# More unread matmuls in TensorE's gaps between the first tile's attention output and the first expert matmul

## The chip, the cores and the metric

One core of one Trainium2 chip. The metric is device time in microseconds (us). A "run" below is one execution of a kernel; each carries its time, its span from the first to the last instruction, and the mean granted clock of TensorE over that span (1.000 is full).

## The reference

Inputs are q, k, v of shape (8 batches, 8 heads, 576 tokens, 64), two norm weights, and two expert matrices of 512 x 2048 and 2048 x 512. In short:

```python
kv  = einsum('bhsd,bhse->bhde', k, v)            # no softmax
out = einsum('bhsd,bhde->bhse', q, kv)
x   = out / sqrt(mean(out**2, -1) + 1e-6) * g_norm      # per head, then heads side by side: 512 wide
xn  = (x - mean(x)) / sqrt(var(x) + 1e-6) * g_ln
y   = x + relu(xn @ w_ch1) @ w_ch2
```

The kernel works on 36 tiles of 128 tokens. A tile goes through: attention output (TensorE), squares and their sums, normalisation and centring (ScalarE, VectorE), a transpose to xT (TensorE), then the two expert products (TensorE).

## The kernel before: the parts that matter

The kernel first makes a plan: every piece of work is a step with an engine, an estimated length and its dependencies, and a small simulation in Python orders the steps. The instructions are then written in that order, with data dependencies guarded by semaphores. After the plan is made, the gaps of TensorE before the first expert matmul are filled with matmuls of a zeroed tile, whose result nobody reads:

```python
def idle_mm(count):
    if "idle" not in blk[0]:
        blk[0]["idle"] = psum.tile([128, 512], f32, tag="mm", name="idle_ps", bufs=BANKS["mm"])
    for _ in range(count):
        nc.tensor.matmul(blk[0]["idle"][:, 0:128], lhsT=blank, rhs=blank, start=True, stop=True)

order = run_plan()
first_mm = min(s.start for s in order if s.main)      # "main": the expert matmuls
pe_end, idle = WARM_FROM, {}
for s in order:
    if s.eng != "PE":
        continue
    if s.start <= first_mm:
        gap = s.start - pe_end                        # as planned, not as measured
        if s.start <= kv_first.start:
            idle[id(s)] = int(gap / 0.107 + 0.5)
        elif gap > 0.3 and not s.main and (s not in urgent or gap > 0.45):
            idle[id(s)] = int((0.6 if s not in urgent or gap > 1.2 else 0.45) * gap / 0.056)
    pe_end = s.start + s.occ
for s in order:
    if id(s) in idle:
        idle_mm(idle[id(s)])                          # unread matmuls just ahead of the step
    s.fn()
```

The first tile of q comes in slots. GpSimd issues their loads between those of the expert weights; the third slot is turned on TensorE (L427) between the two halves of the first tile's own transpose (L586):

```python
pool_load(("q", 0, 1), load_slot(qp[0], q, 0, 1), rate1)
load_w(0, 1)
pool_load(("q", 0, 2), load_slot(qp[0], q, 0, 2), rate1)      # the third slot
load_w(1, 1)
load_w(2, 1)
# ... cut ...
```

## Time and profile before

| | before |
|---|---|
| median of the first 3 runs | 293.42 us (292.99 to 294.43) |
| profiled span | 291.3 us |
| TensorE busy | 283.6 us, 97% |
| first expert matmul | 17.21 us |
| first long run of expert matmuls (64) | 18.95 us |
| unread matmuls | 90, of them 34 after 12 us |

A busy TensorE includes the unread matmuls and the drain of each burst, so its share says nothing about useful work in the first 17 us. The start times of the real matmuls, and the time in brackets before them, do.

### The profile page before, as it was taken

To read this page: it belongs to the slowest core of one execution; us is meant where nothing else is said; L and a number is where in the kernel's file an instruction comes from. 1 tells how busy PE (TensorE), PEld (TensorE's weight loads), DVE (VectorE), ACT (ScalarE), POOL (GpSimd) and SP (SyncE) were. 2 spreads that over 40 slices of the span, in tenths; PEclk is the share of its full clock that TensorE was granted. 3 is DMA by queue.
4 is the path that set the end of the run, shared out by engine and by line. 5 is a ranking of instruction groups with operands and counts; after the bars stand their busy time and mean duration, and the time that the engine had idled before them with its cause. 6 is when DMAs were issued, how large, how long until landed. Compare 5 with 4: busy or idle time off the path is not lost.

```text
span 291.3 us, 5178 instructions
## 1 busy us (share of the span) xinstructions
PE 283.6 (97%) x2046; PEld 162.1 (56%) x2074; DVE 165.0 (57%) x362; ACT 142.6 (49%) x288; POOL 66.7 (23%) x93
## 2 busy tenths in 40 slices
PE   8899999999999999999999999999999999999995
PEld 6779845977645445444544445444544444444444
DVE  2696039487973997557755775477557755320022
ACT  2379954788756512761276126612761177017400
POOL 8974231007309006304060406000000000000000
PEclk9999999999999999999999999999999999999999
DMA  6999999948999998996999399922101210120012
GB/s 95 184 198 205 204 199 179 244 83 96 182 222 94 170 138 141 169 181 140 160 96 188 76 201 96 180 73 92 54 18 56 90 54 18 56 88 20 2 72 73
DMA packets 108332, 35.60 MB, mean 122 GB/s; under 512 B 87059, under 2 KB 103827, under 8 KB 108308
## 3 DMA queue, kind: packets, MB, share of 16 engines
q0 software_dynamic: 72624, 18.35, 66.0%
q1 hardware_dynamic: 35540, 16.85, 25.9%
q8 instruction: 16, 0.26, 0.4%
q14 instruction: 8, 0.07, 0.1%
q10 hardware_dynamic: 144, 0.07, 0.1%
HBM read 36.70 MB, written 9.44 MB: 158 GB/s over the span
## 4 chain that ended last, share of the span: by engine, by line
PE 85%; DMA 7%; POOL 6%; issue 1%; ACT 0%; DVE 0%; POOLq 0%
PE mm_ps L670 41%; PE mm_ps L651 33%; DMA qb<-in_q_dram 7%; PE mm_ps L636 5%; PE out_ps L491 3%; PE kv_ps L468 2%; POOL qp L277 1%; POOL w L361 1%; POOL vb L256 1%; POOL kb L256 1%; PE xT_ps L586 1%; POOL w L363 1%; PE qT_ps L427 0%; ACT qp L407 0%; POOL identity masks.py:197 0%
## 5 line engine op out<-in xcount | busy, mean ns | idle before, releaser
L670 PE MATMUL mm_ps<-w,m 128*128 128x512 bf16 (+2 forms) x592 | 128.1, 367 | 0.7
L651 PE MATMUL mm_ps<-xT,w 128*128 128x512 bf16 x436 | 100.0, 379 | 0.6
L658 ACT ACTIVATE m<-mm_ps 128x512 bf16<-128x512 f32 x112 | 66.8, 597 | 50.8 <-PE mm_ps L651 48.5
L670 PEld LDWEIGHTS <-m 128*128 128x128 bf16 x608 | 57.2, 98 | 60.6
L651 PEld LDWEIGHTS <-w 128*128 128x128 bf16 x448 | 43.1, 98 | 48.8
L526 DVE TENSOR_REDUCE ss<-sq 128x8 f32<-128x512 f32 (+1 forms) x37 | 24.8, 669 | 48.2 <-ACT sq L517 48.1
L677 DVE SCALAR_TENSOR_TENSOR x<-mm_ps,rstd,x 128x512 f32<-128x512 f32 (+2 forms) x38 | 27.3, 720 | 40.6 <-PE mm_ps L670 40.5
L517 ACT ACTIVATE sq<-out_ps 128x512 f32<-128x512 f32 (+1 forms) x37 | 21.6, 584 | 45.4 <-PE out_ps L491 45.4
L636 PE MATMUL mm_ps<-xT,w 128*128 128x128 bf16 x512 | 30.6, 219 | 0.0
L636 PEld LDWEIGHTS <-w 128*128 128x128 bf16 x512 | 29.2, 98 | 0.9 <-DMA w<-in_moe_w_ch_dram 0.2
L579 DVE SCALAR_TENSOR_TENSOR xc<-x,mv,gl 128x512 bf16<-128x512 f32 (+1 forms) x38 | 27.3, 723 | 1.2
L521 DVE TENSOR_TENSOR xg<-out_ps,gn 128x512 f32<-128x512 f32 x34 | 23.2, 683 | 0.2
L757 POOL COPY mark<-xT 128x1 bf16<-128x1 bf16 x15 | 7.5, 497 | 58.1 <-DMA xT<-xc 52.6
L643 ACT ACTIVATE m<-mm_ps 128x512 bf16<-128x512 f32 x32 | 18.4, 596 | 3.1 <-PE mm_ps L636 2.9
L530 ACT ACTIVATE rms<-ss,eps_attn 128x8 f32<-128x8 f32 (+1 forms) x37 | 11.1, 300 | 14.4 <-DVE ss L526 14.3
L557 DVE TENSOR_TENSOR x<-xg,inv 128x512 f32<-128x512 f32 x24 | 16.6, 692 | 0.8
L573 DVE BATCH_NORM_STATS2 stats<-x 128x6 f32<-128x512 f32 x24 | 16.6, 690 | 0.5
L491 PEld LDWEIGHTS <-qT 128*128 128x128 bf16 x160 | 11.4, 98 | 6.4 <-ACT qT L407 0.2
L491 PE MATMUL out_ps<-kv_pack,qT 128*128 128x128 bf16 x160 | 14.5, 219 | 0.2
L479 DVE CAST kv_pack<-kv_ps 64x256 bf16<-64x256 f32 x14 | 5.9, 422 | 11.9 <-PE kv_ps L468 11.8
L468 PEld LDWEIGHTS <-kp 128*128 128x128 bf16 (+1 forms) x168 | 10.5, 100 | 2.4 <-DMA vb<-in_v_dram 0.4
L468 PE MATMUL kv_ps<-vb,kp 128*128 128x128 bf16 (+1 forms) x144 | 11.0, 223 | 0.5 <-DMA vb<-in_v_dram 0.5
(69 smaller groups left out, 182.8 us busy)
## 6 DMA issues: line engine op xcount, KB each, us to landing
out_dram<-x SPq DMA_DIRECT2D x35, 256.0 KB, 2.5
w<-in_moe_w_ch_dram POOLq DMA_DIRECT2D x8, 512.0 KB, 12.3
vb<-in_v_dram POOLq DMA_DIRECT2D x6, 512.0 KB, 10.9
kp<-in_k_dram POOLq DMA_DIRECT2D x5, 512.0 KB, 9.5
qp<-in_q_dram POOLq DMA_DIRECT2D x5, 512.0 KB, 10.2
qb<-in_q_dram POOLq DMA_DIRECT2D x2, 512.0 KB, 18.1
qp<-in_q_dram POOLq DMA_DIRECT2D x10, 64.0 KB, 9.2
kb<-in_k_dram POOLq DMA_DIRECT2D x2, 288.0 KB, 5.6
```

Of the source, the lines that this page charges most:

```text
L468: nc.tensor.matmul(ps[:, hp, :], lhsT=kp[b % 2][p, t, 2 * hp:2 * hp + 2, :].rearrange("p h d -> p (h d)"), rhs=(v5[b % 2][:, 2 * hp:2 * hp ...
L491: nc.tensor.matmul(o3[:, hp, :], lhsT=att[b]["qT"][:, 4 * t + hp, :], rhs=kv_pack[b % 3][:, hp, :], start=(i == 0), stop=(i == len(bs) - 1))
L517: nc.scalar.activation(sq[:, h0:h1, :], st[n]["ps", h0][:, h0:h1, :], func=AF.Square)
L521: nc.vector.tensor_mul(xg[:, h0:h1, :], st[n]["ps", h0][:, h0:h1, :], gn.to_broadcast([128, h1 - h0, D]))
L526: nc.vector.tensor_reduce(ss[:, h0:h1, :], st[n]["sq"][:, h0:h1, :], axis=AX.X, op=ALU.add)
L579: nc.vector.scalar_tensor_tensor(xc[:, f0:f1], in0=st[n]["x"][:, f0:f1], scalar=blk[m]["mv"][:, i, 0:1], in1=gl[:, f0:f1], op0=ALU.subtrac ...
L636: nc.tensor.matmul(ps[:, d, :], lhsT=w1[c][:, kk, d * 128:(d + 1) * 128], rhs=blk[m]["xT"][:, kk, i * 128:(i + 1) * 128], start=(kk == 0), ...
L643: nc.scalar.activation(st[n]["m1"][:, c, :, :], st[n]["m1ps", c], func=AF.Relu)
L651: nc.tensor.matmul(ps, lhsT=w1[c][:, kk, d * 128:(d + 1) * 128], rhs=blk[m]["xT"][:, kk, :], start=(kk == 0), stop=(kk == nKm - 1))
L658: nc.scalar.activation(blk[m]["m1", c][:, d, :], blk[m]["m1ps", g], func=AF.Relu)
L670: nc.tensor.matmul(st[n]["m2ps", f0], lhsT=m1_piece(n, c, d), rhs=w2[c][:, d, f0:f1], start=(c == 0 and d == 0), stop=(c == 3 and d == 3))
L677: nc.vector.scalar_tensor_tensor(x[:, f0:f1], in0=st[n]["m2ps", f0], scalar=blk[m]["rstd"][:, i, :], in1=x[:, f0:f1], op0=ALU.mult, op1=AL ...
```

## The change

Its intent is to keep TensorE busier between the first tile's attention output and the first expert matmul, in the hope that this keeps its clock up.

```diff
             if s.start <= kv_first.start:
                 idle[id(s)] = int(gap / 0.107 + 0.5)
+            elif s.start > 12 and gap > 0.2:
+                idle[id(s)] = int(0.75 * gap / 0.056)
             elif gap > 0.3 and not s.main and (s not in urgent or gap > 0.45):
```

## The prediction

The bound of the first rival: its 3.2 us is the sum of 1.5 us for slow matmuls ahead of the expert stream and of 1.7 us for a stretch at half clock within it. The forecast, 293.4 us, contains neither; "3.2" returns in the ranges as the largest gain of a rival.

> **What bounds the kernel now.** I read the page first (the busy shares and the chain that ended last), then the list of TensorE's instructions in order of time for the stretch that the change touches, then the groups by form in two windows for the clock. The times of before are 293.42 us as the median of three runs, 292.99 to 294.43; the profiled span is 291.3 us, so about 2 us lie outside the span.
>
> The page, parts 1 and 4:
>
> ```profile
> PE 283.6 (97%) x2046; PEld 162.1 (56%) x2074; DVE 165.0 (57%) x362; ACT 142.6 (49%) x288; POOL 66.7 (23%) x93
> PE 85%; DMA 7%; POOL 6%; issue 1%; ACT 0%; DVE 0%; POOLq 0%
> ```
>
> TensorE is busy for 97% of the span and carries 85% of the chain. So the kernel is TensorE's stream of real matmuls, and it can get shorter only where that stream starts earlier, runs at a higher clock, or waits less. The 13% of DMA and GpSimd in the chain are its first part: in order of time, the chain is on GpSimd's issue of loads until 19.19 us, then on a load of q until 38.73, and from there on TensorE. The change touches nothing of that first part: it sits between 11.9 and 17.0 us, before the first expert matmul (L636) at 17.21.
>
> TensorE in that stretch (start, length, engine, line, operation, count; in square brackets the idle time before it and what ended it):
>
> ```profile
> 11.93 0.44 PE L1011 MATMUL idle_ps<-blank 128*128 128x128 bf16 x5
> 12.44 0.29 PE L491 MATMUL out_ps<-kv_pack,qT 128*128 128x128 bf16 x2
> ...
> 13.31 0.66 PE L1011 MATMUL idle_ps<-blank 128*128 128x128 bf16 x9
> 13.99 0.38 PE L491 MATMUL out_ps<-kv_pack,qT 128*128 128x128 bf16 x4
> ...
> 15.90 0.40 PE L427 MATMUL qT_ps<-identity,qp 128*128 128x128 bf16 x4
> 16.53 0.29 PE L586 MATMUL xT_ps<-identity,xc 128*128 128x128 bf16 x2 [0.23 <-DVE xc L579]
> 16.65 0.39 PE L1011 MATMUL idle_ps<-blank 128*128 128x128 bf16 x4
> 16.98 0.40 PE L491 MATMUL out_ps<-kv_pack,qT 128*128 128x128 bf16 x4
> 17.21 1.06 PE L636 MATMUL mm_ps<-xT,w 128*128 128x128 bf16 x16
> 18.27 0.68 PE L586 MATMUL xT_ps<-identity,xc 128*128 128x128 bf16 x4
> 18.95 3.75 PE L636 MATMUL mm_ps<-xT,w 128*128 128x128 bf16 x64
> ```
>
> The lengths include the drain of the last matmul: nine unread ones take 0.66 us, which is 8 pitches of 0.056 plus one duration of about 0.22. So an unread matmul costs 0.056 us of TensorE's issue here, and the engine is free for the next instruction 0.056 us after the last one started. Between the end of the unread ones and the next real matmul there is a pause at nearly every place: VectorE and ScalarE, who make the first tile's normalised x, set the pace.
>
> Is the array at its full clock there? The same unread matmul in two windows, 4.5 to 7.5 us and 12 to 17.2 us (count, busy, mean ns):
>
> ```profile
> L1011 PE MATMUL idle_ps<-blank 128*128 128x128 bf16 x27 | 3.1, 313 | 0.0
> ...
> L1011 PE MATMUL idle_ps<-blank 128*128 128x128 bf16 x34 | 3.0, 219 | 0.0
> ```
>
> 313 ns each in the first, at a pitch of 0.106 us (27 of them in 3.06 us: 26 pitches and one duration); 219 ns each in the second, at a pitch of 0.056. The step comes at about 8 us, inside the first key-value product, and no group of 128-column matmuls after it has a mean above 224 ns. The page's PEclk row reads full in both windows, so it is no witness for this gate; the durations are.
>
> [...]
>
> **The change part by part.** Only the rule that gives the number of unread matmuls per gap differs: from 12 us of the plan's own clock on, 0.75 of each planned gap above 0.2 us is filled, where it was 0.45 or 0.6 of those above 0.3. The plan is made before these numbers, so nothing else can move. The two instruction lists bear it out: with the unread matmuls taken out, the order and the waits are the same on all five engines. TensorE gets 20 more unread matmuls (each with its weight load), 40 instructions. Nothing is removed, no buffer or semaphore is added.
>
> Cost on TensorE: 20 x 0.056 = 1.1 us of issue. What of it lies in pauses? For each place: when the unread ones are through before (first start + n x 0.056), when the next real matmul starts before, and what is added:
> - 11.93 + 5 x 0.056 = 12.21; next at 12.44, when ScalarE's copy of qT (12.02 to 12.39) is there: 0.23 free. Added 4 = 0.22. Just fits.
> - 12.79 + 5 x 0.056 = 13.07; next at 13.20, after ScalarE's square (to 13.15): 0.13 free. Added 1 = 0.06. Fits.
> - 13.31 + 9 x 0.056 = 13.81; next at 13.99, after VectorE's first half of x (13.52 to 13.93): 0.18 free. Added 2 = 0.11. Fits.
> - 14.21 + 4 x 0.056 = 14.43; next at 14.77, after VectorE's second half of x: 0.34 free. Added 2 = 0.11. Fits.
> - 14.99 + 4 x 0.056 = 15.21; next at 15.54, after VectorE's centred x, xc (15.00 to 15.48): 0.33 free. Added 3 = 0.17. Fits.
> - 15.66 + 3 x 0.056 = 15.83; next at 15.90: 0.07 free. Added 1 = 0.06. Just fits.
> - A new place, after the transpose of q at 15.90 (through at 16.12); next at 16.53, after the second half of xc (16.00 to 16.48): 0.41 free. Added 5 = 0.28. Fits.
> - 16.65 + 4 x 0.056 = 16.87; next at 16.98, after a ScalarE copy that ends at 16.92: 0.11 free. Added 2 = 0.11. Just fits.
>
> Sum of the additions 4+1+2+2+3+1+5+2 = 20, and every one lies in its pause. On the path: 0 us, with perhaps 0.02 to 0.05 at each of the three tight places. Even such a slip doesn't last. The first would delay a square on ScalarE that starts at 12.77, when the engine's previous work ends anyway. The last would delay the first expert matmuls, and behind those TensorE waits again: the transposes at 18.27 and about 18.66 wait for VectorE's xc of the second tile (VectorE is busy without a break from 16.00 to 17.50, not waiting for TensorE), and the long run at 18.95 waits 0.17 for the load of the next weights. From 18.95 on the stream starts when that load lands, whatever happened at 17.
>
> Gain: the clock can't rise above full. In this execution it had been full for 4 us when the change begins, so there is nothing to win. TensorE's busy time in the page should rise, because what were pauses now counts as busy; that is no work done.
>
> **The rivals.**
> - *The clock drops in some executions, and filling prevents it.* For it: [...] between 14 and 17 us TensorE streams only 11 to 14 matmuls per us, 60 to 80% of the pitch. One of the three runs of before is 1.0 us above the median. Against it: the profiled run has no slow matmul after 8 us, in spite of those pauses. Worth at most, as an estimate: about 30 real matmuls between 12 and 17.2 at 0.05 more, 1.5 us, [...] 3.2 us, 1.1%, in a run that had it. That would give 290 at the very best; as a median over runs, most of which didn't have it, a few tenths.
> - *The added matmuls come in the way.* If the three tight places overrun by 0.05 each, and nothing behind absorbs it: 0.15 us, 293.6. If all 20 were in series: 1.1 us, 294.5; at half clock 2.1 us, 295.5. Against it: the pauses above, and the waits for VectorE and for weights at 18.27 and 18.95.
> - *The end is set elsewhere.* The load of q that the chain follows from 19.19 to 38.73 is issued by GpSimd, whose list doesn't change; a shift of TensorE by hundredths can't move it. This says 0 as well.
>
> **Range and chances.** The middle is the median of before, 293.4 us. What remains is the spread between runs (292.99 to 294.43) and a few tenths either way from the first two rivals: 292.6 to 294.4 should hold it 8 times in 10. A change of 2% is 5.9 us; the largest gain and the largest loss of the rivals are 3.2 and 2.1 us, so both outer chances are left for what I haven't thought of: 0.01 each.
>
> **What would show it right or wrong.** In the changed profile: 110 unread matmuls with the same shortest and median duration; those after 12 us still at 219 ns; the first expert matmul at 17.2 (within 0.05) and the long run of 64 at 18.95; the brackets before the real matmuls at L506 and L586 smaller or gone; TensorE busy a few tenths of a us more; and from 19 us on the same chain. I would be wrong if the first expert matmul moved by more than 0.2 us and the end followed it, if matmuls of 300 ns appeared or went in the stretch, or if repeated runs of both kernels differed by more than 1 us in their medians.

## The result, and the profile after

| | before | after |
|---|---|---|
| median of 6 runs | 293.26 us (292.95 to 294.43) | 293.21 us (292.81 to 293.40) |
| ratio | | 0.9991, 95% interval 0.9973 to 1.001 |
| profiled span | 291.3 us | 291.6 us |
| first expert matmul | 17.21 us | 17.84 us |
| first long run of 64 | 18.95 us | 19.05 us |

A ratio is the mean time of one kernel's fast runs over that of the other's of the same rounds, so it is not quite the ratio of the medians.

The page of the kernel after, part 1, and its unread matmuls between 12 and 17.2 us, by form (count, busy us, mean ns, idle before):

```profile
PE 285.8 (98%) x2094; PEld 163.6 (56%) x2094; DVE 164.9 (57%) x362; ACT 142.4 (49%) x288; POOL 66.2 (23%) x93
```

```profile
L1011 PE MATMUL idle_ps<-blank 128*128 128x128 bf16 x49 | 4.0, 219 | 0.0
```

The busy time rose by 2.2 us, more than the 1.1 us that 20 unread matmuls cost (20 x 0.056), and it is no gain: the pauses are now counted as busy, and the trace holds 48 more matmul records, 28 of them real ones that the trace of before had lost (592 and 436 matmuls at L670 and L651, where 608 and 448 weight loads are recorded). I had expected a few tenths. The unread ones still take 219 ns: full clock, as before.

TensorE of the kernel after in the stretch that the prediction shows of before (start, length, engine, line, operation, count, idle before):

```profile
11.89 0.67 PE L1011 MATMUL idle_ps<-blank 128*128 128x128 bf16 x9
12.41 0.29 PE L491 MATMUL out_ps<-kv_pack,qT 128*128 128x128 bf16 x2
...
13.28 0.78 PE L1011 MATMUL idle_ps<-blank 128*128 128x128 bf16 x11
13.96 0.38 PE L491 MATMUL out_ps<-kv_pack,qT 128*128 128x128 bf16 x4
...
16.54 0.40 PE L427 MATMUL qT_ps<-identity,qp 128*128 128x128 bf16 x4 [0.52 <-DMA qp<-in_q_dram]
16.77 0.44 PE L1011 MATMUL idle_ps<-blank 128*128 128x128 bf16 x5
17.05 0.28 PE L586 MATMUL xT_ps<-identity,xc 128*128 128x128 bf16 x2
17.16 0.50 PE L1011 MATMUL idle_ps<-blank 128*128 128x128 bf16 x6
17.61 0.40 PE L491 MATMUL out_ps<-kv_pack,qT 128*128 128x128 bf16 x4
17.84 1.06 PE L636 MATMUL mm_ps<-xT,w 128*128 128x128 bf16 x16
18.74 0.39 PE L586 MATMUL xT_ps<-identity,xc 128*128 128x128 bf16 x4
19.05 3.75 PE L636 MATMUL mm_ps<-xT,w 128*128 128x128 bf16 x64
```

The fills of 9 and 11 fit: the real matmuls behind them start 0.03 us earlier than before. Then the third slot of q comes late: its transpose waits 0.52 us for a load and starts at 16.54 instead of 15.90. That load is issued by GpSimd, whose list did not change; nothing of the change can delay it. But the fill behind it is now in the way. VectorE's second half of xc was there at 16.43, yet five unread matmuls stand ahead of the transpose that reads it (17.05), which costs 0.28 us. In an execution with the load in time they had lain in a pause. The first expert matmul moves by 0.63 us, the run of 64 by 0.10 only, because before had waited there for VectorE and for weights anyway (18.27, 18.66 and 18.95).

So the medians agree with the prediction. What they don't show is in the last row of each spread: of six runs of before one took 294.43 us, of six after none took over 293.40.

### The profile page after: what moved, and what is told of

It is laid out like the page before. It is cut to its first block, busy times and chain, and to the rows that moved or that the text cites. A ratio compares the mean times of both kernels' runs of the same rounds, so it can differ in the third digit from the quotient of the medians.

```text
span 291.6 us, 5246 instructions
## 1 busy us (share of the span) xinstructions
PE 285.8 (98%) x2094; PEld 163.6 (56%) x2094; DVE 164.9 (57%) x362; ACT 142.4 (49%) x288; POOL 66.2 (23%) x93
## 4 chain that ended last, share of the span: by engine, by line
PE 90%; DMA 6%; POOL 2%; issue 0%; ACT 0%; DVE 0%; POOLq 0%
PE mm_ps L670 42%; PE mm_ps L651 33%; PE mm_ps L636 8%; DMA qT<-qp 3%; PE out_ps L491 3%; DMA qp<-in_q_dram 3%; PE kv_ps L468 2%; PE xT_ps L586 1%; POOL qp L277 1%; POOL vb L256 1%; POOL kb L256 1%; PE qT_ps L427 1%; POOL w L361 0%; PE idle_ps L1011 0%; POOL identity masks.py:197 0%
## 5 line engine op out<-in xcount | busy, mean ns | idle before, releaser
L670 PE MATMUL mm_ps<-w,m 128*128 128x512 bf16 (+2 forms) x608 | 129.6, 368 | 0.0
L651 PE MATMUL mm_ps<-xT,w 128*128 128x512 bf16 x448 | 100.6, 379 | 0.0
L670 PEld LDWEIGHTS <-m 128*128 128x128 bf16 x608 | 57.2, 98 | 60.6
L651 PEld LDWEIGHTS <-w 128*128 128x128 bf16 x448 | 43.1, 98 | 48.9
L757 POOL COPY mark<-xT 128x1 bf16<-128x1 bf16 x15 | 6.7, 448 | 57.8 <-DMA xT<-xc 51.6
L491 PEld LDWEIGHTS <-qT 128*128 128x128 bf16 x160 | 11.4, 98 | 6.6 <-DMA qT<-qp 0.5
L491 PE MATMUL out_ps<-kv_pack,qT 128*128 128x128 bf16 x160 | 14.7, 219 | 0.4 <-DMA qT<-qp 0.4
```

The costliest lines, as they stand in the source:

```text
L491: nc.tensor.matmul(o3[:, hp, :], lhsT=att[b]["qT"][:, 4 * t + hp, :], rhs=kv_pack[b % 3][:, hp, :], start=(i == 0), stop=(i == len(bs) - 1))
L651: nc.tensor.matmul(ps, lhsT=w1[c][:, kk, d * 128:(d + 1) * 128], rhs=blk[m]["xT"][:, kk, :], start=(kk == 0), stop=(kk == nKm - 1))
L670: nc.tensor.matmul(st[n]["m2ps", f0], lhsT=m1_piece(n, c, d), rhs=w2[c][:, d, f0:f1], start=(c == 0 and d == 0), stop=(c == 3 and d == 3))
```

## The experiments

Twelve experiments ran, each six times, in three calls of four; three of them are the same kernel, the one after. A call shares 11 runs of the kernel before on the same chip; the three calls were on three different chips. All outputs were correct.

**First call: take the fill away, or overdo it.** Theory: the unread matmuls after 12 us neither gain nor cost. Rivals: they hold the clock; they are in the way.

No unread matmul after 12 us:

```diff
-            elif gap > 0.3 and not s.main and (s not in urgent or gap > 0.45):
+            elif s.start < 12 and gap > 0.3 and not s.main and (s not in urgent or gap > 0.45):
```

> The kernel before, with no unread matmul at all after 12 us (34 fewer than before, 54 fewer than after). My theory: they neither gain nor cost; VectorE and ScalarE set the pace there, and the array stays at full clock on the real matmuls. Then: ratio to before 0.998 to 1.002, real matmuls of the stretch still 219 ns, first expert matmul at 17.2 (17.8 if the third slot of q lands late again). Rival 'the clock': without them the array is gated, real matmuls of 312 ns appear between 12 and 21 us, and the kernel is 1.5 to 3 us slower (0.5 to 1%). Rival 'in the way': they cost 0.056 us each on the path, and the kernel is faster than before by 0.3 to 1.9 us.

Measured: 294.68 us median, ratio 1.0033 (1.0006 to 1.0059). All six runs have a mean granted clock of 0.987 to 0.994. My theory in the form "they gain nothing" is refuted: without them the clock is lost every time. In the profiled run the third slot of q landed late (transpose at 17.27), and the clock was halved from about 17.3 us (0.65 granted from 17 to 18 us, 0.50 from 18 to 20).

No unread matmul after the first key-value product:

```diff
-            elif gap > 0.3 and not s.main and (s not in urgent or gap > 0.45):
+            elif False and gap > 0.3 and not s.main and (s not in urgent or gap > 0.45):
```

> The kernel before, with no unread matmul after the first key-value product at 8.6 us (51 fewer). From 8.6 to 12 us only 20 real matmuls of 0.056 us are left in 3.4 us, a third of the pitch, so this is where the rival 'the clock' has its best chance: matmuls of 312 ns from about 12 us on, [...] and +2 to +3.5 us. If the clock holds even so, my theory in its strong form stands (no unread matmul after warming is needed): ratio 0.998 to 1.002. I expect the clock to fall here, 65 to 35.

Measured: 294.23 us, ratio 1.0028 (0.9998 to 1.0058). The clock fell in at least four of six runs (0.98 to 0.988); the profiled one was at half from 12.7 to 19.5 us (0.50 granted in every window from 14 to 19). The size was below my +2 to +3.5 us: in the profiled run most of the half clock lay where TensorE waits for VectorE anyway, and the expert stream, from 17.86 us on, saw only the end of it.

Factor 1.5 in place of 0.75:

```diff
-                idle[id(s)] = int(0.75 * gap / 0.056)
+                idle[id(s)] = int(1.5 * gap / 0.056)
```

> The change with factor 1.5 in place of 0.75: 111 unread matmuls after 12 us (57 more than after, 77 more than before), so that they overrun every pause. My theory says that what does not fit costs: about 57 x 0.056 = 3.2 us later at the first expert matmul (about 20.4), of which the waits at 18.3 to 19 and at 39 to 60 us take 0.5 to 1.5 back: 1.7 to 2.7 us slower than before (ratio 1.006 to 1.009). If the start of the expert stream does not matter for the end (rival 'the end is set elsewhere', by the loads of q at 38.73): ratio below 1.002.

Measured: 294.53 us, ratio 1.0030 (1.0005 to 1.0054); no run lost the clock (0.998 the lowest). First expert matmul at 20.08, close to the 20.4 expected. Against those nine runs of before in this call that kept their clock, the mean span is longer by 1.1 us (292.77 against 291.64), so less reached the end than I expected.

Forty unread matmuls ahead of the first expert matmul:

```diff
+        if s.main and s.start == first_mm:
+            idle_mm(40)
         if id(s) in idle:
```

> The changed kernel, and 40 unread matmuls right ahead of the first expert matmul: 40 x 0.056 = 2.24 us on TensorE behind all of the first tile's work. It measures how much of a delay at 17.2 us reaches the end. First expert matmul at 19.5 to 20.1; the long run of 64 starts at about 20.6 in place of 18.95; end later by 1.2 to 1.7 us (ratio 1.004 to 1.006) if the stream from there is dense, below 0.5 us if a later wait (for the loads of q or the transposes by DMA) sets the pace anyway.

Measured: 295.61 us, ratio 1.0066 (1.0039 to 1.0093), clock kept. First expert matmul at 19.79, run of 64 at 20.90. The mean span is longer by 1.7 us (293.30 against 291.64). The times are longer still by 0.5 us, as three of the six runs spent 2.5 to 3.2 us outside the span; why stays open. Both runs together say that the start of the expert stream does matter: a run of 64 that starts about 2 us later (20.90 here, 21.20 in the overfilled kernel, 18.95 in before) costs 1.7 and 1.1 us at the end. An unread matmul that doesn't fit in a pause is paid for in part.

**What this call changed.** The 11 runs of before carry their clocks, too: nine have 0.998 or more, but two have 0.994, and took 294.67 and 295.30 us. A mean of 0.994 over 292 us is a loss of 0.006 x 292 = 1.75 us of full clock, or 3.5 us at half. So before does lose its clock, in some runs; the single profiled run that I read had kept it. New theory: the thicker fill prevents that. I call a run "lost" below 0.997. (Values of 0.997 to 0.999 come from the end: in two copies of the kernel after, the clock is full until 280 us and 0.94 and 0.91 in the last 12 us, of which TensorE is busy for 8.18 and 7.77.)

**Second call: the kernel after three times over, and half the fill.**

> The changed kernel as it is, for its spread. The last runs changed my mind on the clock: in 2 of 11 runs of the kernel before the mean granted clock was 0.994 in place of 1.000, and these took 294.67 and 295.30 us against a median of 293.44; none of the 6 first runs of the changed kernel was below 0.999. New theory: the fill of before is too thin in some executions, in which the clock is halved for some us and 1.2 to 1.9 us are lost; the thicker fill prevents that. Then none of the 18 runs of the three copies falls below 0.997, while about 2 of 11 of before do again; the medians are the same within 0.3 us, and only the worst run of before is longer. Rival (chance): the changed kernel drops as often, 3 of 18.

> Second copy of the changed kernel, as for the first: no run with a clock below 0.997 by the theory, about one of six by the rival. Ratio to before 0.998 to 1.000.

> Third copy of the changed kernel, as for the first. The profiles of the three also show how far the first expert matmul moves with the landing of the third slot of q alone: between 17.2 and 18.0 us, with the spans not following it one to one.

Measured: medians 293.37, 293.36 and 293.20 us, ratios 0.9981, 0.9986 and 0.9979, each interval just reaching over 1. None of the 18 runs was lost; of the 11 runs of before in the same call, three were (294.49 to 294.81 us). In the three profiles the first expert matmul came at 17.40, 17.34 and 17.77, and the spans were 291.6, 291.2 and 291.3: they don't follow it. In all three profiles the whole stretch was already about that much late before the third slot is used: the attention output (L491) that before starts at 12.44 starts here at 12.61, 12.58 and 12.95. So my expectation that the third slot alone moves it was wrong.

Half the unread matmuls after 12 us, in the kernel before:

```diff
                 idle[id(s)] = int((0.6 if s not in urgent or gap > 1.2 else 0.45) * gap / 0.056)
+                if s.start > 12:
+                    idle[id(s)] //= 2
```

> The kernel before with half its unread matmuls after 12 us (15 in place of 34). If the fill decides how often the clock is lost, this lies between before (2 of 11 runs) and no fill at all (6 of 6 runs at 0.987 to 0.994): 2 to 5 of 6 runs below 0.997, and a mean 0.4 to 1.0 us above before (ratio 1.0015 to 1.0035). If it were chance, its share would be that of before, 1 of 6.

Measured: 294.59 us, ratio 1.0018 (0.9989 to 1.0046), three of six runs lost, as expected. Its profiled run was one of them. TensorE of the half fill, windows of 1 us (busy share and count for TensorE, its weight loads, VectorE, ScalarE, GpSimd, then the granted clock, DMA share, GB/s):

```profile
16.00:17.00 1.00, 0.10 (x2) 0.00 (x0) 0.89 (x3) 0.57 (x2) 1.00 (x2) 1.00 1.34 204
17.00:18.00 1.00, 0.54 (x8) 0.45 (x8) 0.90 (x4) 0.10 (x1) 1.00 (x2) 1.00 1.23 203
18.00:19.00 1.00, 0.55 (x7) 0.47 (x6) 0.83 (x2) 0.76 (x2) 1.00 (x2) 0.56 1.24 208
19.00:20.00 1.00, 1.00 (x12) 1.00 (x10) 0.19 (x1) 0.60 (x1) 0.06 (x2) 0.50 1.32 200
20.00:21.00 1.00, 1.00 (x12) 1.00 (x11) 1.00 (x2) 0.00 (x0) 0.84 (x1) 0.50 2.04 172
21.00:22.00 1.00, 1.00 (x16) 1.00 (x15) 0.09 (x1) 0.90 (x3) 0.00 (x0) 0.73 1.31 205
```

Here is the loss itself: full until 18.1, half until 21.5. Adding up the missing parts, 2 x (0.44 + 0.50 + 0.50 + 0.27) = 3.4 us at half clock. It comes just when the expert stream begins, and there 12 matmuls start per us instead of the 22 that before has from 20 to 23 us. Ahead of it lies a near-empty us from 16 to 17, for this run, too, had the third slot late:

```profile
15.88 0.22 PE L1011 MATMUL idle_ps<-blank 128*128 128x128 bf16 x1
17.46 0.40 PE L427 MATMUL qT_ps<-identity,qp 128*128 128x128 bf16 x4 [1.36 <-DMA qp<-in_q_dram]
```

**Third call: make the slot late on purpose.** The two profiled runs that lost the clock at 17 to 18 us both had a late slot, so I tested whether that decides it. Half of one weight load was issued ahead of the slot; the order on TensorE, VectorE and ScalarE stayed as it was:

```diff
-    pool_load(("q", 0, 2), load_slot(qp[0], q, 0, 2), rate1)
-    load_w(1, 1)
+    q2_fn, q2_nb = load_slot(qp[0], q, 0, 2)
+    def w11(k0, k1):
+        nc.gpsimd.dma_start(w1[1][:, k0:k1, :], w1_src[:, k0:k1, 512:1024])
+    pool_load(("q", 0, 2), (lambda: (w11(0, 2), q2_fn()), q2_nb), rate1)
+    pool_load(("w", 1, 1), (lambda: w11(2, 4), 512 * 512 * 4), 355.0)
```

In the kernel before:

> The kernel before, with half of one weight load issued ahead of the third slot of q, so that this slot lands about 1.4 us later in every execution (at 17 to 18 us in place of 16 to 16.5); all lists but GpSimd's stay as they are. Of the profiled runs so far, the two that lost the clock about 17 us (no late fill, half fill) are the two in which this slot landed after 17.2, with 1.3 us of idle TensorE before it. Theory L: the kernel before loses the clock in those executions in which the slot happens to land late; then here 4 to 6 of 6 runs fall to 0.994 or less, mean 294.5 to 295.5. Rival (phase): [...] a late slot matters little: 1 to 2 of 6.

Measured: 294.84 us, six of six runs lost, where the rival gave 1 to 2. In this call the kernel before itself lost 5 of 11; with equal chances all six would fall among the lost in about 4 of 100 draws.

In the kernel after:

> The changed kernel with the same late slot. If the 20 further unread matmuls protect against the late slot, 0 to 1 of 6 runs lose the clock, mean 293.8 to 294.5, and shorter than the late before by 0.5 to 1.2 us. If they don't (the gap itself, about 1.3 us, is no better filled: one more unread matmul ahead of it, five right after), it loses the clock as often as the late before, and then the 24 of 24 runs of the changed kernel without a loss would be due to something else.

Measured: 293.65 us, two of six runs lost (295.38 and 294.91 us), a mean 0.9 us below the late before (294.03 against 294.95). So the fill lowers the risk of a late slot, but does not remove it: I expected 0 to 1 lost. (Two of six against six of six would come by chance in about 3 of 100 draws.) The two profiled runs side by side, first the late before, then the late after (lines are shifted by 3 from the other kernels; L639 is the first expert matmul):

```profile
15.20 0.28 PE L589 MATMUL xT_ps<-identity,xc 128*128 128x128 bf16 x2 [0.17 <-DVE xc L582]
15.32 0.33 PE L1014 MATMUL idle_ps<-blank 128*128 128x128 bf16 x3
17.55 0.40 PE L430 MATMUL qT_ps<-identity,qp 128*128 128x128 bf16 x4 [1.90 <-DMA qp<-in_q_dram]
...
19.03 1.91 PE L639 MATMUL mm_ps<-xT,w 128*128 128x128 bf16 x16
```

```profile
15.46 0.28 PE L589 MATMUL xT_ps<-identity,xc 128*128 128x128 bf16 x2
15.58 0.39 PE L1014 MATMUL idle_ps<-blank 128*128 128x128 bf16 x4
17.75 0.40 PE L430 MATMUL qT_ps<-identity,qp 128*128 128x128 bf16 x4 [1.78 <-DMA qp<-in_q_dram]
...
19.06 1.06 PE L639 MATMUL mm_ps<-xT,w 128*128 128x128 bf16 x16
```

The idle time in front of the slot is nearly the same, 1.90 and 1.78 us. The first expert matmuls start at the same time, yet 16 of them take 1.91 us in one and 1.06 us in the other: half clock against full. The added matmuls did not fill the long gap; they made the time around it busier.

Whether the busier time around it kept the clock in this run is not shown, for the two runs also differ in where, by the count that follows, the clock could change. In the profiles that lost it, the clock stayed at half for 3.4 us (the half fill, no unread after 12 us, the late before) or 6.8 us (none after the key-value product). In the half fill it went to full at 7.89 us, fell at 18.13, 10.24 us or three times 3.41 later, and rose at 21.54, another 3.41 later. So I counted in stretches of 3.41 us from the change to full clock, at 7.96 us in the late before and at 10.45 in the late after (by the length of its matmuls). That the clock changes only at the ends of such stretches is an assumption of mine. The long gap then lies in one stretch of the late before, and the clock falls at the end of that stretch, 18.20; in the late after the end of a stretch, 17.27, cuts the gap in two. First the stretch of the late before, then the two of the late after (columns as in the windows above):

```profile
14.79:18.20 3.41, 1.34 (x20) 0.91 (x17) 3.20 (x9) 0.79 (x3) 3.36 (x7) 1.00 1.52 188
```

```profile
13.86:17.27 3.41, 2.05 (x30) 1.55 (x27) 3.05 (x9) 1.17 (x3) 3.26 (x7) 1.00 1.52 190
17.27:20.68 3.41, 2.93 (x51) 2.81 (x52) 1.98 (x7) 1.88 (x5) 3.41 (x5) 1.00 1.44 196
```

In the four profiles that lost the clock, the stretch that ended in the fall has TensorE busy for 1.08 us (no unread after 12 us), 1.34 (the late before), 1.46 (the half fill) and 1.90 (none after the key-value product). The stretches of full clock that I counted beside them in the first 25 us have more: the least is the 2.05 us above, in before it is 2.73 and in the first profile of after 2.89. From 14.79 to 18.20 us, where the stretch of the late before lies, the late after is busy for 1.63 us. Had its stretches lain there, it would have lost the clock by this count, which is no more than an estimate; two of its six runs did lose it. By this count the late slot, the fill and the place of the stretches act together. It was made after the fact from four falls, and no run tests it.

The kernel after with the late slot, and the long gap filled as well:

```diff
+        if s is behind_first:
+            idle_mm(24)
         if id(s) in idle:
```

> The changed kernel with the late slot, and 24 more unread matmuls ahead of the transpose that waits for it (24 x 0.056 = 1.34 us), so that TensorE is idle nowhere. The clock should hold in all 6 runs; what is left against before is the late slot alone: first expert matmul about 18.3 to 18.9, mean 293.5 to 294.3. Against the late changed kernel it tells what an idle of 1.3 us costs by the clock.

Measured: 293.57 us, ratio 0.9991 (0.9959 to 1.0023), none of six lost. With the clock kept, the late slot itself costs 0.5 us (293.46 against 292.96, the mean of the six runs of before in this call that kept it), even though the first expert matmul came at 19.49 in its profile.

No unread matmul at all:

```diff
         if id(s) in idle:
-            idle_mm(idle[id(s)])
```

> The kernel before without any unread matmul (90 fewer). It sizes what all of them are worth[...]. About 60 real matmuls of the first tile at 0.106 and their chain of waits longer by 0.1 us at each of some 8 hops, and some 40 to 60 expert matmuls at half clock: 1.5 to 3.5 us slower than before (ratio 1.005 to 1.012), clock 0.98 or less. If the gate did not matter: ratio 1.000 or less.

Measured: 294.57 us, ratio 1.0027 (0.9992 to 1.0062), so by these runs all 90 together are hardly worth more than the 34 after 12 us. The recorded clock is 0.998 to 1.000, against my expectation of 0.98 or less; but the durations say otherwise. No unread at all, 4 to 20 us, by form:

```profile
L468 PE MATMUL kv_ps<-vb,kp 96*128 96x128 bf16 x24 | 3.1, 307 | 3.4 <-DMA vb<-in_v_dram 3.0 <-DVE qT L409 0.5
L427 PE MATMUL qT_ps<-identity,qp 128*128 128x128 bf16 x12 | 2.1, 311 | 0.7 <-DMA qp<-in_q_dram 0.7
...
L636 PE MATMUL mm_ps<-xT,w 128*128 128x128 bf16 x16 | 1.9, 314 | 0.0
```

Everything up to and including the first 16 expert matmuls runs at the slow duration (means of 292 to 314 ns, against 219 at full clock), and the record shows full clock. The transposes among them (L427) take 311 ns; those of before from 12 to 17.2 us (L427 and L586) take 220 and 224 ns on the mean. The recorded clock shows a fall (0.50 in the half fill), but not the slow state in which these kernels begin (in before, 313 ns with 1.00 recorded from 4.5 to 7.5 us): the trace's record starts with the first change, here at 20.0 us, and what comes before counts as full. The trace of the late after has no such record at all, so its 1.000 rests on the lengths of its matmuls alone. A recorded 1.000 is thus weaker evidence than a recorded fall.

**All runs whose clock is recorded:**

| kernel | unread after 12 us | runs | lost | mean us |
|---|---|---|---|---|
| before | 34 | 33 | 10 | 293.80 |
| after (first result and three copies) | 54 | 24 | 0 | 293.30 |
| half | 15 | 6 | 3 | 294.41 |
| none after 12 us | 0 | 6 | 6 | 294.64 |
| none after the key-value product | 0 | 6 | 4 at least | 294.34 |
| none at all | 0 | 6 | 0 recorded, but slow from the start | 294.52 |
| overfilled | 111 | 6 | 0 | 294.55 |
| forty ahead of the first expert matmul | 94 | 6 | 0 | 295.62 |
| late slot, before | 34 | 6 | 6 | 294.95 |
| late slot, after | 54 | 6 | 2 | 294.03 |
| late slot, after, gap filled | 78 | 6 | 0 | 293.46 |

The 10 lost runs of before have a mean of 294.86 us, its other 23 of 293.34: a loss costs 1.5 us. Had before and after lost equally often, 10 lost runs among these 57 would all fall to before in about 2 of 1000 draws. That pools three calls on different chips; in the second call alone, where both ran on the same chip (3 of 11 against 0 of 18), it is about 5 of 100. Not every long run is a recorded loss: 294.39 and 294.58 us of before and 294.40 of after came with a clock of 1.000. Counted by time alone, over 294.3 us, it is 12 of 33 against 1 of 24. No kernel tried here is faster than the changed one.

## Why the prediction was right, and where its reasons were not

*The time: right.* 293.21 us against 293.4, within the range. Some of that is the choice of the median, which hardly sees the runs that lose the clock: over all runs with a recorded clock the medians are 293.44 before and 293.31 after.

*"Every one lies in its pause": right where the loads come in time.* In the three copies every fill fitted to within some hundredths of a us. It is a statement about one execution, though: in the profiled run of after, the slot was 0.6 us late and the five new unread matmuls behind it cost 0.28 us on the way to the first expert matmul.

*"The first expert matmul at 17.2 (within 0.05)": wrong, without harm.* It came between 17.34 and 17.84 in four profiles of after. In the first, the late load of q moved it, and of its 0.63 us the new fill behind that load took 0.28. In the three copies the shift was there from 12.6 us on, and what the fills can have added is 0.05 us or less (17.40, 17.34 and 17.77 are 0.19, 0.13 and 0.56 later than in before, the start of the stretch 0.17, 0.14 and 0.51). My condition for being wrong, a move of over 0.2 us that the end follows, was badly chosen: the spans of these four lie between 291.2 and 291.6 with no relation to it.

*"So there is nothing to win": this step failed.* It held for runs that keep their clock: 293.34 us before, 293.30 after. But I took one profiled run for all, and put the lost clock among the rivals as a matter of few runs. It happened in 10 of 33. As means over all runs the change wins 293.80 - 293.30 = 0.5 us (0.2%; 293.83 - 293.36, the same, in the second call alone), all of it by lost runs that no longer occur. Each single comparison has 1 within its interval. The rival's size was right in kind ("a few tenths"), and its bound of 3.2 us for one lost run was twice the measured 1.5: 3.4 us at half clock, as measured in the half fill, take 1.7 us, which is what the term came to, and nearly all of the loss. The other term, 1.5 us for slow matmuls ahead of the stream, is not there in the profiled losses of the half fill and of the late before, as the clock falls when that part is nearly over (at 18.13 and 18.20, the stream starts at 18.93 and 19.03).

*"The end is set elsewhere": wrong as a general rule.* The load of q that the chain follows until 38.73 us did not absorb a start of the expert stream about 2 us later: 1.1 and 1.7 us reached the end. (A small misreading besides, which changes nothing: VectorE is not busy without a break from 16.00 to 17.50 us in before; it pauses for 0.14 us at 16.67.)

*"The page's PEclk row ... is no witness for this gate": half wrong.* It shows the falls of the clock (0.50 in the half fill), and misses the slow beginning (1.00 where matmuls take 313 ns). Had I known, one look at the clocks of several runs of before would have told me more than the pauses of one.

*What stays open.* With the slot made late, before lost its clock in every run (six of six, against 5 of 11 as it is). That its own 10 lost runs are those with a late slot is likely but not shown: none of them was profiled. Nor is the count by stretches of 3.41 us tested, nor how much of the 0 of 24 is due to slots that happened to land in time; the late after, with two of six, is not safe.

## What to carry to other kernels

Filler work is to be judged by the worst runs and by the recorded clock of each run, not by one profile and a median: here the median did not move while 10 of 33 runs lost 1.5 us. Filler put by a plan at fixed places fitted here while the loads landed as planned. In the first profile of after, where one landed late, the filler in front of that wait cost nothing, as TensorE still waited 0.52 us for the load behind it; the filler behind it stood in the way for 0.28 us. Filler that overran its pauses was paid for in part: an expert stream that started about 2 us later cost 1.1 and 1.7 us at the end.
